# An RWKV attention with a token and channel mixer on one core: other costs in the planner, u turned by two wide transposes or by TensorE, and the row of w spread by a matmul

## The chip, the cores and the metric

The kernel runs on one core of a Trainium2 chip. The metric is the device time of one execution in microseconds (us). The five engines of the core are TensorE (PE in the profile), VectorE (DVE), ScalarE (ACT), GpSimd (POOL) and SyncE (SP). Each has its own queue and works through it in order. SP computes nothing here: it issues DMAs. PSUM is the memory into which TensorE writes, SBUF the one from which the engines work.

## The reference

Two parts, the output of the first being the input of the second (4 batches, 8 heads, 768 tokens, 48 numbers a head, so 384 to a token):

```python
for t in range(S):                       # attention, per batch and head
    cur = einsum('bhd,bhe->bhde', u * kt, vt)
    y[:, :, t] = einsum('bhd,bhde->bhe', rt, state + cur)
    state = w * state + einsum('bhd,bhe->bhde', kt, vt)
...
h  = max(xt @ w_tok1, 0) @ w_tok2        # mixer over the tokens, xt: x with tokens last
u  = x + h.T
h2 = max(u @ w_ch1, 0) @ w_ch2           # mixer over the channels
out = u + h2
```

Two things bear the name u: the small input `u` (8 x 48) of the attention, and the tensor u = x + h.T of the mixer. "u turned" is the second: the channel mixer needs u with its 384 channels on the partitions.

## The kernel before

**Attention.** The recurrence is done in blocks of 128 tokens. A block of one batch is a *unit*; there are 24 of them, 6 to a batch, units 0 to 5 being batch 0. For a unit, k, r and v (192 KB each) are loaded by SP's queue (`load`). k and r are multiplied by powers of w (`kp`, `rp`, on POOL or DVE, by the tables `wn` and `wp`), v is cast on ACT (`vb`). Both products, held side by side in `kpr` (128 x 1024), have to be turned so that the head's numbers lie on the partitions: by TensorE for units 0 to 11 (`trk`, `trr`: four transposes each into PSUM, then the copy `rk` on ACT, 128 x 1024), by one DMA transpose from SP's queue for units 12 to 23 (`turn_unit`; the tuple `turned`). Then come the scores (`at`, 8 matmuls into two PSUM tiles), their masking (`AT`, on DVE; in units 0 to 5 the second half is first copied out by ACT, `raw`, and masked from SBUF, `ATr`), the diagonal (`pr` on DVE, `pg` on TensorE, `adgp`, `yd`), the state (`kv` on TensorE, `S`), the outputs (`yS`, `y` on TensorE) and their sum `x` on DVE.

**Mixer.** Once a batch has all its x: `hid` (12 matmuls), `hr`, `bk` (12 matmuls into `hT_ps`), `us` (u, six adds on DVE, tiles of 128 x 384), and u turned. In batch 0 (`pe_turn`) TensorE turns it (`tu`: three transposes to a block, `uT`: the copy out of PSUM); in batches 1 to 3 six DMA transposes to a batch, each 128 x 384, go out on SP's queue (`uTd`). Then for either half of the batch 36 matmuls `z` (into `z_ps`, their moving operand being the turned u, 384 columns in a row), the maximum `zr`, 36 matmuls `h` (into `h_ps`), the last sum `os` (tile `osb`) and the store. The four weights come by POOL's queue, each after a certain unit's `rp` (`wafter`).

**What sets the order.** `graph` lists all steps with the engines that could do each, the time that the step is planned to keep an engine busy and the time after which its result is seen, a rank, and what must come before it. `Plan.run` plays this forward: whenever an engine is free, the ready step of lowest rank is given to it. Steps are then emitted in the order of their planned starts, and every engine keeps that order (`tc.keep_in_program_order`). So planned costs change no computation; they decide which engine takes a step that two can do, and in which order each queue holds its work. A step that is late in fact holds up what stands behind it in its queue. The factor `cold` stretches the planned TensorE time of units 0 to 5 and of batch 0's `hid`.

**Start.** ACT's queue loads w, repeated on all partitions (`w_bc`, 192 KB); ACT makes from it lnw and the tables. TensorE runs eight matmuls on zeros (`idle_ps`, `warm=8`). SP loads k, r, v of unit 0 and then the rows of w and u as a small tile (`rows`), which a matmul turns (`wu`, in f32); then the loads of unit 1 follow.

All instructions have one line in the profile (L338, the wrapper that keeps the order), so groups are told apart by their tiles.

Of the kernel before, what the change touches and what calls it, by code (L numbers as in the profile page):

```python
# [13 lines left out]
f32 = mybir.dt.float32  # L14
# [9 lines left out]
T = 128  # L24
# [20 lines left out]
class Plan:  # L45
# [3 lines left out]
    def __init__(self, banks, busy_until, in_flight):  # L49
        self.steps, self.banks, self.busy_until, self.in_flight = [], banks, busy_until, in_flight  # L50
# [20 lines left out]
    def run(self):  # L71
# [5 lines left out]
        while todo:  # L77
# [4 lines left out]
            while again:  # L82
                again = False
                for s in sorted(open_, key=lambda s: (s.rank, s.ready)):
# [40 lines left out]


# [7 lines left out]
def graph(do, cfg):  # L134

    p = Plan(4, cfg.get("busy_until", dict(ACT=3.0, DVE=3.3, POOL=3.6)), cfg.get("in_flight", 8))
# [9 lines left out]
    tables = {0: p.add("tables0", [("ACT", 1.6, 1.75)], rank=-100, emit=do("tables", 0))}  # L146
    setup = tables[0]
    for g in (1, 2):
        tables[g] = p.add(f"tables{g}", [("ACT", 1.05, 1.2)], [setup], rank=g - 0.6, emit=do("tables", g))

    wu = p.add("wu", [("PE", 0.6, 0.8)], rank=0.05, emit=do("wu"))
# [16 lines left out]
    def weight(i, after):  # L168
        s = p.add(f"i:w{i}", [("POOL", 0.9, 1.0, True)], after, rank=-50, emit=do("weight", i))
        took = cfg.get("wtime", (3.3, 3.0, 7.0, 7.8))[i]  # L170
        wx[i] = p.transfer(f"x:w{i}", s, took, took + 1.0, -1.0)

    p.wait(wu, [loads["v", 0]])
# [3 lines left out]
    for u in range(NU):  # L177
# [10 lines left out]
        rp = p.add(f"rp{u}", [POOL2, DK], [loads["r", u], tab, old], rank=r + 0.1, emit=do("rp", u))  # L188
# [52 lines left out]
    for b in range(B):  # L241
# [9 lines left out]
        uT = []  # L251
        for c in range(C):
# [5 lines left out]
            else:  # L258
                s = p.add(f"i:uT{b}_{c}", [("SP", 1.25, 1.3)], [us], rank=-3000 + c, emit=do("uTd", b, c))
                uT.append(p.transfer(f"x:uT{b}_{c}", s, 0.4, 1.3, 0.0))  # L260
        for sg in range(2):
# [7 lines left out]
            for si in range(3):  # L269
# [5 lines left out]
                s = p.add(f"i:o{b}_{c}", [("SP", 0.35, 0.4)], [s], rank=-1500, emit=do("out", b, c))  # L275
                stores.append(p.transfer(f"x:o{b}_{c}", s, 0.6, 1.8, 0.0))
# [20 lines left out]
def kernel(  # L297
# [52 lines left out]
    u_bc = const.tile([128, dm], f32, name="u_bc") if wide else None  # L350
    act.preload_act_table_set("natural_log_exp_and_others")

# [4 lines left out]
    for _ in range(CFG.get("warm", 0)):  # L357
        pe.matmul(idle_ps, idle[:, 0:128], idle, start=True, stop=True)


    rows = const.tile([2 * HP, 2, P], f32, name="rows")
    dve.memset(rows, 1.0)
# [44 lines left out]
    def tables(eng, g):  # L407
        if g == 0:
            act.activation(lnw, w_bc, Ln)
        act.activation(wn[:, g, :], lnw, Exp, scale=iota[:, 1, g:g + 1])  # L410
        act.activation(wp[:, g, :], lnw, Exp, scale=iota[:, 0, g:g + 1])
# [295 lines left out]
```

## Time and profile before

| | |
|---|---|
| median of 3 runs | 188.04 us (187.84 to 188.58) |
| the profiled execution | 188.54 us, its span 186.8 us |
| TensorE busy | 160.3 us (86%), 1440 matmuls |
| DVE, ACT, POOL busy | 97.1, 85.5, 61.9 us |
| DMA | 27.38 MB, 147 GB/s on average |
| mean granted TensorE clock | 0.982 |

The span runs from the first to the last instruction; 1.74 us of the execution lie around it. A busy TensorE is one with a matmul in its pipe: back to back, the 384-column matmuls start closer together than the duration that the profile gives for one. In a timeline row the first number is the start in us, the second the time to the end of the last instruction of the row; what stands in square brackets is the idle time of the engine before the row and what ended it. SPq is SP's queue, where the time of a row is that of issuing.

### The profile page before, as it was taken

What the parts mean: (1) busy time and instruction counts of PE and PEld (TensorE: products, weight loads), DVE (VectorE), ACT (ScalarE), POOL (GpSimd) and SP (SyncE); (2) the same over time, 40 slices, a digit from 0 to 9 for tenths busy, and PEclk for the clock granted to TensorE, in tenths of its full rate; (3) what the DMA queues carried; (4) which work ended last, traced back from release to release, by engine and by line L of the source; (5) the groups of instructions that cost most, each with busy time, mean ns of one, the idle gap of its engine ahead of it and who ended that gap; (6) DMA issues with size and microseconds to landing.
All of it is one profiled execution on the core that took longest, in us unless ns stands there. A gap on an engine that the chain in (4) does not pass through costs nothing.

```text
span 186.8 us, 3768 instructions
## 1 busy us (share of the span) xinstructions
PE 160.3 (86%) x1440; PEld 99.1 (53%) x1440; DVE 97.1 (52%) x199; ACT 85.5 (46%) x183; POOL 61.9 (33%) x77
## 2 busy tenths in 40 slices
PE   7458778799999999658979899974999999999992
PEld 2346555365666666434546454542656566556650
DVE  3279965650289877951834678734526702102121
ACT  2868555189538642017332473120551290652800
POOL 4208700044087699330185456511501000000000
PEclk9999999999999999979999999998799999999999
DMA  4899999999769899946899999749631352302103
GB/s 96 161 219 215 190 204 200 186 201 214 149 165 197 170 216 159 204 80 125 181 190 208 208 204 241 130 82 210 159 58 42 63 67 91 120 0 88 42 2 126
DMA packets 101690, 27.38 MB, mean 147 GB/s; under 512 B 95528, under 2 KB 101288, under 8 KB 101672
## 3 DMA queue, kind: packets, MB, share of 16 engines
q1 hardware_dynamic: 98520, 23.80, 62.6%
q0 software_dynamic: 3008, 3.15, 10.2%
q10 hardware_dynamic: 144, 0.20, 0.5%
q8 instruction: 11, 0.18, 0.4%
q14 instruction: 7, 0.06, 0.1%
HBM read 20.65 MB, written 4.72 MB: 136 GB/s over the span
## 4 chain that ended last, share of the span: by engine, by line
PE 53%; DVE 13%; DMA 12%; SPq 6%; issue 6%; ACT 4%; POOL 4%; POOLq 0%; DVEq 0%; ACTq 0%
PE h_ps L338 21%; PE z_ps L338 21%; SPq L338 6%; DMA ld_k<-in_k_dram 4%; DVE AT L338 3%; DMA ld_r<-in_r_dram 3%; PE hT_ps L338 3%; PE y_ps L338 3%; POOL kpr L338 2%; DMA ld_v<-in_v_dram 2%; DVE x_b L338 2%; DVE u_sb L338 2%; ACT rk L338 2%; PE at_ps L338 2%; PE tr_ps L338 2%
## 5 line engine op out<-in xcount | busy, mean ns | idle before, releaser
L338 ACT ACTIVATE zr<-z_ps 128x384 bf16<-128x384 f32 x95 | 46.2, 491 | 35.8 <-PE z_ps L338 35.7
L338 PE MATMUL z_ps<-uT,wch 128*128 128x384 bf16 x288 | 56.4, 337 | 1.6 <-DMA uT<-u_sb 1.6
L338 PE MATMUL h_ps<-wch,zr 128*128 128x384 bf16 x288 | 55.2, 326 | 0.0
L338 PEld LDWEIGHTS <-wch 128*128 128x128 bf16 x288 | 27.6, 100 | 19.4 <-issue 4.2
L338 PEld LDWEIGHTS <-zr 128*128 128x128 bf16 x288 | 26.6, 97 | 15.6
L338 POOL TENSOR_TENSOR yd<-vb,adg 128x384 f32<-128x384 bf16 x19 | 15.7, 828 | 45.3 <-ACT adg L338 44.9
L338 DVE TENSOR_TENSOR osb<-u_sb,h_ps 128x384 f32<-128x384 bf16 x24 | 13.0, 550 | 33.8 <-PE h_ps L338 33.7
L338 POOL TENSOR_TENSOR kpr<-ld_k,wn 128x384 bf16<-128x384 f32 x21 | 21.3, 1015 | 24.0 <-DMA ld_k<-in_k_dram 18.7
L338 DVE TENSOR_TENSOR AT<-at_ps,mask 128x512 bf16<-128x512 f32 x42 | 27.6, 683 | 2.1 <-PE at_ps L338 1.9
L338 POOL TENSOR_TENSOR kpr<-ld_r,wp 128x384 bf16<-128x384 f32 x20 | 20.6, 1028 | 9.1 <-DMA ld_r<-in_r_dram 5.7
L338 DVE TENSOR_TENSOR pr<-rk 128x512 bf16<-128x512 bf16 x24 | 12.2, 512 | 15.0 <-DMA rk<-kpr 11.3
L338 DVE TENSOR_TENSOR x_b<-y_ps,yd 128x384 bf16<-128x384 f32 x24 | 13.3, 553 | 11.8 <-PE y_ps L338 6.8
L338 PEld LDWEIGHTS <-kpr 128*128 128x128 bf16 x176 | 13.5, 113 | 9.7 <-DVE kpr L338 3.4
L338 PEld LDWEIGHTS <-rk 48*128 48x128 bf16 (+1 forms) x272 | 11.1, 101 | 14.0 <-DMA rk<-kpr 6.4
L338 ACT CAST vb<-ld_v 128x384 bf16<-128x384 f32 x24 | 12.2, 510 | 12.7 <-DMA ld_v<-in_v_dram 12.7
L338 ACT COPY rk<-tr_ps 128x1024 bf16<-128x1024 bf16 x12 | 12.1, 1010 | 9.6 <-PE tr_ps L338 7.6
L338 PE MATMUL at_ps<-rk 48*128 48x128 bf16 x192 | 10.6, 237 | 5.2 <-DMA rk<-kpr 4.1
L338 PE MATMUL tr_ps<-ident,kpr 128*128 128x128 bf16 x96 | 11.9, 265 | 2.7 <-DVE kpr L338 2.3
L338 DVE TENSOR_TENSOR S<-kv_ps,bm 128x384 bf16<-128x384 f32 x13 | 7.2, 553 | 13.1 <-PE kv_ps L338 10.6
L338 PE MATMUL h_ps<-x_b,wtok 128*128 128x384 bf16 x48 | 12.4, 348 | 1.5 <-DVE x_b L338 1.5
L338 DVE TENSOR_TENSOR u_sb<-x_b,hT_ps 128x384 bf16<-128x384 bf16 x24 | 11.9, 550 | 1.5 <-PE hT_ps L338 1.5
L338 PEld LDWEIGHTS <-wtok 128*128 128x128 bf16 x96 | 8.8, 100 | 6.9 <-issue 2.6
(58 smaller groups left out, 109.1 us busy)
## 6 DMA issues: line engine op xcount, KB each, us to landing
ld_k<-in_k_dram SPq DMA_DIRECT2D x24, 192.0 KB, 3.6
ld_r<-in_r_dram SPq DMA_DIRECT2D x24, 192.0 KB, 4.0
ld_v<-in_v_dram SPq DMA_DIRECT2D x24, 192.0 KB, 3.7
out_dram<-osb SPq DMA_DIRECT2D x24, 192.0 KB, 2.0
wch<-in_moe_w_ch_dram POOLq DMA_DIRECT2D x2, 1152.0 KB, 14.4
wtok<-in_moe_w_tok_dram POOLq DMA_DIRECT2D x2, 384.0 KB, 6.6
uT<-u_sb SPq DMA_TRANSPOSE x18, 2.4
w_bc<-in_w_dram ACTq DMA_DIRECT2D x1, 192.0 KB, 3.9
```

What stands on the lines that cost most here:

```text
L338: return lambda *args, **kw: tc.keep_in_program_order(f(*args, **kw))
```

## The change

- **Planned costs.** A load's issue costs SP 0.60 us in the plan (0.45 before) and its transfer 1.01 us, seen after 2.1 (0.93, 1.9); the transfers of a unit's DMA transpose, of the weights and of the stores get other times as well. ACT, DVE and TensorE are planned busy until 3.85, 3.6 and 5.0 us. `cold` is 1.7 in place of 1.0. The tables are split into single steps (`lnw`, `wn`, `wp`), and `rp` waits for `wp` alone.
- **Batch 0.** `raw` is empty: both halves of the scores are masked on DVE straight from PSUM. Weights are issued after units 4, 5, 5, 5 (3, 4, 5, 5 before).
- **u turned.** In batch 1 by TensorE, as in batch 0 (`pe_turn=(0, 1)`). In batches 2 and 3 by two DMA transposes to a batch, each of 128 x 1152 (half a batch). The tile `uT` is laid out by blocks, so the 384 columns that a `z` matmul reads are three pieces of 128, 384 apart.
- **Units 12 and 13** are turned by TensorE (`turned=range(14, 24)`).
- **Start.** w comes as one row (1.5 KB) on one partition and is spread by a matmul in f32 with a row of ones (`w_ps`, 128 x 384); lnw reads PSUM. The `rows` are issued on ACT's queue ahead of its table load. Two matmuls on zeros stand ahead of `w_ps` and ten behind it.
- A function `fill` is added, and not used with this `CFG`.

```diff
-    p = Plan(4, cfg.get("busy_until", dict(ACT=3.0, DVE=3.3, POOL=3.6)), cfg.get("in_flight", 8))
+    p = Plan(4, cfg.get("busy_until", dict(ACT=3.85, DVE=3.6, POOL=3.6, PE=5.0)), cfg.get("in_flight", 8))
...
-                s = p.add(f"i:{nm}{i}", [("SP", 0.45, 0.6)], fetched[-1:], rank=-1000 + n, emit=do("load", nm, i))
+                s = p.add(f"i:{nm}{i}", [("SP", 0.6, 0.65)], fetched[-1:], rank=-1000 + n, emit=do("load", nm, i))
...
-                loads[nm, i] = p.transfer(f"x:{nm}{i}", s, 0.93, 1.9, 0.0)
+                loads[nm, i] = p.transfer(f"x:{nm}{i}", s, 1.01, 2.1, 0.0)
...
-            s = p.add(f"i:t{u}", [("SP", 1.25, 1.3)], [kp, rp], rank=-2000, emit=do("turn_unit", u))
-            rk = p.transfer(f"x:t{u}", s, 1.0, 2.2, 0.0)
+            s = p.add(f"i:t{u}", [("SP", 1.35, 1.4)], [kp, rp], rank=-2000, emit=do("turn_unit", u))
+            rk = p.transfer(f"x:t{u}", s, 1.56, 2.2, 0.0)
...
-                s = p.add(f"i:uT{b}_{c}", [("SP", 1.25, 1.3)], [us], rank=-3000 + c, emit=do("uTd", b, c))
-                uT.append(p.transfer(f"x:uT{b}_{c}", s, 0.4, 1.3, 0.0))
+                some.append(us)
+                if c % G == G - 1:
+                    s = p.add(f"i:uT{b}_{c}", [("SP", 1.35, 1.4)], some, rank=-3000 + c, emit=do("uTd", b, c // G))
+                    uT += [p.transfer(f"x:uT{b}_{c}", s, 1.75, 2.4, 0.0)] * G
+                    some = []
...
-    wafter={0: 3, 1: 4, 2: 5, 3: 5},
+    wafter={0: 4, 1: 5, 2: 5, 3: 5},
     hold={6: ("rp", 5)},
-    turned=range(12, 24),
-    raw=range(6),
+    turned=range(14, 24),
+    pe_turn=(0, 1),
     kr0=0.2, yd0=0.1,
-    cold=1.0,
-    warm=8,
+    cold=1.7,
...
-    w_bc = const.tile([128, dm], f32, name="w_bc")
-    act.dma_start(out=w_bc, in_=w.rearrange("h d -> (h d)")[None, :].to_broadcast([128, dm]))
+    row = const.tile([1, 2, dm], f32, name="row")
+    rows = const.tile([2 * HP, 2, P], f32, name="rows")
+    dve.memset(rows, 1.0)
...
+            act.dma_start(out=row[:, j, :], in_=src.rearrange("h d -> (h d)")[None, :])
+    for j, src in enumerate((w, u)):
+        act.dma_start(rows[j * HP:j * HP + HP, :, 0:D], src.rearrange("(a q) d -> a q d", q=2))
...
+    warm(CFG.get("warm", (2, 10))[0])
+    pe.matmul(w_ps, ones, row[:, 0, :], start=True, stop=True)
+    warm(CFG.get("warm", (2, 10))[1])
...
-            for j, src in enumerate((w, u)):
-                sp.dma_start(rows[j * HP:j * HP + HP, :, 0:D], src.rearrange("(a q) d -> a q d", q=2))
...
-    def uTd(eng, b, c):
-        sp.dma_start_transpose(M[b]["uT"][:, :, ts(c, 128)], M[b]["u"][:, c, :])
+    def uTd(eng, b, sg):
+        half = slice(sg * G, sg * G + G)
+        sp.dma_start_transpose(M[b]["uT"][:, half].rearrange("p c m t -> p (c m) t"),
+                               M[b]["u"][:, half].rearrange("p c n -> p (c n)"))
...
-            pe.matmul(M[b]["z", sg, j], wch1[:, m, ts(j, 128)], M[b]["uT"][:, m, ds(sg * 384, 384)],
+            pe.matmul(M[b]["z", sg, j].rearrange("p (c t) -> p c t", c=G), wch1[:, m, ts(j, 128)], M[b]["uT"][:, sg * G:sg * G + G, m, :],
```

## Rows read from the trace of the kernel before

**Rows 1.** The page, part 2: TensorE's busy tenths in 40 slices of the span

```profile
PE   7458778799999999658979899974999999999992
```

**Rows 2.** Windows: length, busy us of PE, PEld, DVE, ACT, POOL, granted clock, DMA share, GB/s

```profile
76.70:82.30 5.60, 2.15 (x37) 1.39 (x36) 4.93 (x10) 0.33 (x2) 2.61 (x3) 0.93 0.67 139
82.30:88.00 5.70, 5.49 (x32) 2.95 (x32) 0.56 (x1) 3.55 (x8) 0.00 (x0) 0.77 0.55 106
88.00:95.00 7.00, 4.78 (x68) 3.27 (x69) 4.27 (x8) 2.88 (x8) 2.07 (x3) 1.00 0.85 175
95.00:124.50 29.50, 28.11 (x279) 16.65 (x277) 19.35 (x38) 10.30 (x26) 16.24 (x18) 1.00 0.97 189
124.50:133.00 8.50, 5.00 (x46) 2.70 (x43) 3.00 (x7) 2.13 (x5) 1.65 (x2) 0.80 0.88 189
133.00:183.20 50.20, 50.01 (x341) 30.03 (x337) 13.76 (x27) 22.23 (x47) 2.79 (x4) 1.00 0.24 64
```

**Rows 3.** Timeline of TensorE, 82 to 95 us

```profile
82.34 2.08 PE L338 MATMUL z_ps<-uT,wch 128*128 128x384 bf16 x6 [1.56 <-DMA uT<-u_sb]
84.56 3.27 PE L338 MATMUL z_ps<-uT,wch 128*128 128x384 bf16 x18
...
94.74 0.33 PE L338 MATMUL kv_ps<-vb,kpr 128*128 128x96 bf16 x4 [1.64 <-ACT vb L338]
```

**Rows 4.** Timeline of SP's queue, 77 to 128 us

```profile
77.27 7.71 SPq L338 DMA_TRANSPOSE uT<-u_sb  x6
...
88.96 0.70 SPq L338 DMA_DIRECT2D ld_v<-in_v_dram  x1
...
116.91 8.33 SPq L338 DMA_TRANSPOSE uT<-u_sb  x6
125.34 2.63 SPq L338 DMA_TRANSPOSE rk<-kpr  x2
```

**Rows 5.** Timeline of TensorE, 128 to 132 us

```profile
128.62 0.40 PE L338 MATMUL at_ps<-rk 48*128 48x128 bf16 x8 [3.44 <-DMA rk<-kpr]
...
129.37 3.08 PE L338 MATMUL z_ps<-uT,wch 128*128 128x384 bf16 x9
```

**Rows 6.** The chain that ended last, at 148 us: start, length, what

```profile
148.49 5.36 PE z_ps L338 x33
```

**Rows 7.** Timeline of TensorE, transposes between other matmuls, 58 us

```profile
57.93 0.40 PE L338 MATMUL tr_ps<-ident,kpr 128*128 128x128 bf16 x4
58.16 0.65 PE L338 MATMUL z_ps<-uT,wch 128*128 128x384 bf16 x3
```

**Rows 8.** Timeline of the start: SP's queue and TensorE, 1 to 8 us

```profile
1.27 3.60 PE L338 MATMUL idle_ps<-idle 128*128 128x512 bf16 x8 [1.27 <-DVE idle L338]
...
1.95 2.65 SPq L338 DMA_DIRECT2D ld_v<-in_v_dram  x1
...
6.20 0.45 SPq L338 DMA_DIRECT2D ld_k<-in_k_dram  x1
...
7.55 0.56 PE L338 MATMUL wu_ps<-ident_f,rows 8*128 8x8 f32 x2 [2.68 <-DMA rows<-in_u_dram]
```

**Rows 9.** Groups by form: the masking of scores and its copy (count, busy, mean ns)

```profile
L338 DVE TENSOR_TENSOR AT<-at_ps,mask 128x512 bf16<-128x512 f32 x42 | 27.6, 683 | 2.1 <-PE at_ps L338 1.9
...
L338 ACT CAST raw<-at_ps 128x512 bf16<-128x512 f32 x6 | 3.5, 587 | 1.3 <-PE at_ps L338 1.2
L338 DVE TENSOR_TENSOR AT<-raw,mask_b 128x512 bf16<-128x512 bf16 x6 | 2.5, 424 | 0.2 <-ACT raw L338 0.2
```

**Rows 10.** Timeline of TensorE: the same eight matmuls at 27 and at 31 us

```profile
27.17 0.61 PE L338 MATMUL at_ps<-rk 48*128 48x128 bf16 x8 [0.68 <-ACT rk L338]
...
31.13 0.40 PE L338 MATMUL at_ps<-rk 48*128 48x128 bf16 x8 [0.23 <-ACT rk L338]
```

**Rows 11.** Timeline of TensorE: four matmuls of two columns, and the next row

```profile
110.40 0.24 PE L338 MATMUL kv_ps<-UW,pr 128*128 128x2 bf16 x4
110.50 0.65 PE L338 MATMUL z_ps<-uT,wch 128*128 128x384 bf16 x3
```

More of the change, by code (lines that the diff above doesn't have):

```diff
@@ L110, in run @@
                         banks[i], held[s.name] = float("inf"), i
+                        self.used.append([now, float("inf"), s.name])
                     for g in s.give:
                         banks[held.pop(g)] = s.seen
+                        next(x for x in self.used if x[2] == g)[1] = s.seen
                         heapq.heappush(times, s.seen)
@@ L124, in run, with fill @@
         return sorted(self.steps, key=lambda s: s.start)
+    def fill(self, until, least, margin, each, emit):
+        mine = sorted((s for s in self.steps if s.engine == "PE"), key=lambda s: s.start)
+        for a, b in zip(mine, mine[1:]):
+            if b.start > until:
+                break
+            taken = sum(1 for x in self.used if x[0] < b.start and x[1] > a.end)
+            n = int((b.start - a.end - margin) / each)
+            if b.start - a.end >= least and taken < self.banks and n > 0:
+                s = self.add(f"fill{a.name}", [("PE", n * each, n * each)], emit=emit(n))
+                s.engine, s.start, s.end, s.seen = "PE", a.end, a.end + n * each, a.end + n * each
+        return sorted(self.steps, key=lambda s: s.start)
 MM = 0.1625
@@ L169, in weight @@
         s = p.add(f"i:w{i}", [("POOL", 0.9, 1.0, True)], after, rank=-50, emit=do("weight", i))
-        took = cfg.get("wtime", (3.3, 3.0, 7.0, 7.8))[i]
+        took = cfg.get("wtime", (3.0, 2.6, 6.2, 7.7))[i]
         wx[i] = p.transfer(f"x:w{i}", s, took, took + 1.0, -1.0)
-    p.wait(wu, [loads["v", 0]])
     wafter = cfg["wafter"]
@@ L274, in graph @@
                 downs[-1].append(s)
[L275 to L276 removed]
+                s = p.add(f"i:o{b}_{c}", [("SP", 0.57, 0.6)], [s], rank=-1500, emit=do("out", b, c))
+                stores.append(p.transfer(f"x:o{b}_{c}", s, 0.63, 1.8, 0.0))
     rng = random.Random(cfg.get("seed", 0))
@@ L356, with warm @@
     idle_ps = psM.tile([128, 512], f32, name="idle_ps", tag="m")
[L357 to L362, printed above, removed]
+    w_ps = psM.tile([128, dm], f32, name="w_ps", tag="m")
+    def warm(n):
+        for _ in range(n):
+            pe.matmul(idle_ps, idle[:, 0:128], idle, start=True, stop=True)
+    warm(CFG.get("warm", (2, 10))[0])
+    pe.matmul(w_ps, ones, row[:, 0, :], start=True, stop=True)
+    warm(CFG.get("warm", (2, 10))[1])
+    if wide:
+        u_ps = psM.tile([128, dm], f32, name="u_ps", tag="m")
+        pe.matmul(u_ps, ones, row[:, 1, :], start=True, stop=True)
     iota_i = const.tile([128, 2, G], i32, name="iota_i")
@@ L405, with lnw_, wn_, wp_ @@
     wGm = const.tile([128, HP, 2, D], f32, name="wGm")
-    def tables(eng, g):
-        if g == 0:
-            act.activation(lnw, w_bc, Ln)
+    def lnw_(eng):
+        act.activation(lnw, w_ps, Ln)
+    def wn_(eng, g):
         act.activation(wn[:, g, :], lnw, Exp, scale=iota[:, 1, g:g + 1])
+    def wp_(eng, g):
         act.activation(wp[:, g, :], lnw, Exp, scale=iota[:, 0, g:g + 1])
@@ L422, in uw @@
             dve.tensor_mul(UW[half, :, q], wu_sb[half, 0, :], wu_sb[half, 1, :])
+        if wide:
+            dve.tensor_copy(u_bc, u_ps)
     wtok1 = wts.tile([128, 6, dtok], bf16, name="wtok1")
@@ L627, in uT @@
     def uT(eng, b, c):
[L628 removed]
+        to = M[b]["uT"][:, c]
         if eng == "ACT":
@@ L662 @@
     STEPS = {
-        "tables": tables, "wu": wu, "uw": uw, "load": load, "weight": weight, "gd": gd, "wGm": wgm, "kp": kp, "rp": rp,
+        "lnw": lnw_, "wn": wn_, "wp": wp_, "wu": wu, "uw": uw, "load": load, "weight": weight, "gd": gd, "wGm": wgm, "kp": kp, "rp": rp,
         "vb": vb, "ku": ku, "rku": rku, "adg": adg, "yd": yd, "turn_unit": turn_unit,
@@ L672, in do, with fill @@
         return lambda eng: STEPS[kind](eng, *args)
-    for s in graph(do, CFG).run():
+    def fill(eng, n):
+        t = psM.tile([128, 256], f32, name="fill_ps", tag="m")
+        for _ in range(n):
+            pe.matmul(t, idle[:, 0:128], idle[:, 0:256], start=True, stop=True)
+    plan = graph(do, CFG)
+    steps = plan.run()
+    if CFG.get("fill"):
+        first = next(s for s in steps if s.name == "z0_0_0").start
+        steps = plan.fill(first, *CFG["fill"], lambda n: lambda eng: fill(eng, n))
+    for s in steps:
         if s.emit is not None:
```

27 lines of the change are left out of this document (15 added, 12 removed).

## The prediction

> **What bounds the kernel now.** I read first the page's row of TensorE by slices [rows 1]: the reader sees a start of mixed digits, nines from slice 9 on, then two dips, in slices 17 to 21 and in 27 and 28 (a slice is 4.67 us), and nothing but nines from slice 29 until the stores. So TensorE is the bound from about 40 us on, except in those dips; nothing that shortens another engine's work elsewhere can pay. Then I asked for windows around the dips [rows 2]. From 95.0 to 124.5 us TensorE is idle for 1.39 us, from 133.0 to 183.2 for 0.19. From 76.7 to 95 it is idle for 3.45 + 0.21 + 2.22 = 5.88 us, from 124.5 to 133 for 3.50. After each dip the granted clock falls (0.77 and 0.80 as means of the windows), so TensorE is busy and slow there. Last I asked the timelines of TensorE and of SP's queue who ends these waits [rows 3 to 5].
>
> The unit price comes from a stretch without waits: 33 z matmuls in 5.36 us, 0.162 each [rows 6]; the profile's duration of a group is longer by the pipe's drain, 0.65 - 3 x 0.162 = 0.16 us [rows 7].
>
> *First dip (batch 1).* SP issues six transposes of u in a row, 7.71 us, 1.29 each [rows 4]. The first z waits 1.56 us for one [rows 3]. Behind the six stand loads: v that is issued at 88.96 us [rows 4] is what ACT waits for, and TensorE through it, 1.64 us at 94.74 [rows 3]. The 24 z that follow the hole take 2.08 + 3.27 = 5.35 us where 24 x 0.162 + 2 x 0.16 = 4.22 would do: 1.13 lost to the lower clock. Lost in all: 5.88 + 1.13 = 7.0 us.
>
> *Second dip (batch 2).* Again six transposes, 8.33 us, and behind them, at 125.34, two transposes of units [rows 4]; TensorE waits 3.44 us for such a one, and the next nine z take 3.08 us where 9 x 0.162 + 0.16 = 1.62 would do [rows 5]. Lost: 3.50 idle and 1.46 at the lower clock, 5.0 us.
>
> *Batch 3* has six such transposes too, but TensorE is full from 133 us on [rows 2], so they cost nothing.
>
> **The change, part by part.**
>
> *u of batch 1 and units 12 and 13 on TensorE.* Removed from SP: six transposes and two of units, some 10 us of its queue; the loads behind move up by that. Added to TensorE: 18 transposes for u and 16 for the units. Four take 58.16 - 57.93 = 0.23 us of TensorE's time [rows 7], 0.057 each, so 34 x 0.057 = 1.9 us, all on the path, as TensorE is the bound there. Added to ACT: six copies of u and two of 128 x 1024. The nearest row for a copy out of PSUM is 0.587 us for 128 x 512 [rows 9], so 6 x 0.587 + 2 x 1.17 = 5.9 us at most; ACT is idle for 18.3 - 6.8 = 11.5 us of this stretch [rows 2], which hides them. If the plan gives them to DVE there is no such cover: DVE works 4.93 of 5.6 us from 76.7 on [rows 2]. DVE is therefore the next late one once SP is out of the way, and I take not all of the 7.0 but 6.2 (what DVE has free in that window, 0.67, is about what I leave). Ends: 3.5 (only the hole before the first z goes) and 7.0.
>
> *Two wide transposes.* A transpose of a unit moves eight blocks of 128 x 128 and costs SP 2.63/2 = 1.32 us; one of u moves three and costs 8.33/6 = 1.39 [rows 4]. So an issue does not grow with its blocks up to eight, and nine should cost about 1.4: two cost 2.8 us in place of 8.33, and the transposes of units behind them are issued 5.5 us sooner. That is more than the 3.44 us wait that they end, so the hole closes, and the clock does not fall after it. The wide one must wait for three sums u where the narrow one waited for one, and holds all of SP's queue meanwhile: two more operations on DVE, at most 2 x 0.683 [rows 9] = 1.4 us; 5.5 - 1.4 still covers 3.44. I take 4.5 of 5.0; ends 0 (something else arrives late at the same place) and 5.0. Batch 3: nothing, as above.
>
> *Batch 0.* w_bc's 192 KB leave the first loads' way, and two small issues leave SP's queue. Now v of unit 0 takes 2.65 us to issue and the next load comes at 6.20, 1.6 us after that issue ends [rows 8]. The 1.6 are certain; about 2 of the 2.65 may go as well, if w_bc held it up. So units 1 to 5 are loaded 1.6 to 3.6 us sooner. Against it: without `raw` DVE has 6 x (0.683 - 0.424) = 1.6 us more to do in batch 0, ACT 3.5 less [rows 9]; and ten matmuls on zeros stand ahead of unit 0's transposes in TensorE's order. Eight take 3.6 us [rows 8], ten 4.5, behind a spread of w that can't start before its row has landed. The nearest row for that is the small tile's, for which TensorE waits until 7.55 [rows 8]; issued first on ACT it should be there at about 3 us. The f32 matmul of 384 columns lies between 0.28 (half the 0.56 of the two f32 records [rows 8]) and some 2 us (12 x 0.16). So TensorE is free for unit 0 between 7.8 and 9.5 us; now it is at 8.1 (7.55 + 0.56). I take a gain of 1.0 for the start; ends -2.0 and +3.6.
>
> *Costs in the plan.* They change order, not work. What order can still give is the idle time outside the dips, 1.4 us between 95 and 124.5 [rows 2]; what it can take away I bound by the same amount. Weights one unit later and the split tables: within the same bound. I take 0. That the whole first batch is planned 1.7 times slower agrees with the trace: eight scores take 0.61 us at 27 us and 0.40 at 31 [rows 10], and less pipe's drain the ratio is nearer two, so this stretch runs at the lower of the two clock levels (1.2 and 2.4 GHz).
>
> The rule of the Trainium skill that speaks against moving turns to TensorE is in its page "TensorE: Matmul & The Clock Gate", Part 4 (PE-mode transpose): a transpose does not count as activity for the clock as a matmul does. By it, the clock would fall around u of batch 1 and the 1.13 us of rows 3 would stay, 179.3 in place of the forecast. The trace is against it as far as it goes: z right behind transposes runs at its full rate there [rows 7].
>
> **Sum.** 1.0 + 6.2 + 4.5 - 1.9 = 9.8 us. The rows come from an execution of 188.54 us (span 186.8 and 1.74 around it), 0.50 above the median of the runs; a gain is the same against either, so 188.04 - 9.8 = 178.2 us.
>
> **Rivals.**
>
> 1. *The second hole stays.* From 95 to 124.5 the DMA engines are already at a share of 0.97 [rows 2]. If loads for units 18 to 23, wanted some 5 us sooner, can't come sooner, TensorE waits for them where it waited for the transpose. For it: that share; a wide transpose moves the same bytes. Against: between 76.7 and 95 the shares are 0.67, 0.55, 0.85 [rows 2], room for 5.6 x 0.33 + 5.7 x 0.45 + 7 x 0.15 = 5.5 us of transfers. Time: 178.2 + 4.5 = 182.7.
> 2. *The clock is up in batch 0.* If twelve matmuls on zeros that run on into unit 0 without a gap raise the clock and the work behind holds it, each TensorE step of batch 0 is 0.21 us shorter [rows 10]; four steps (transposes, scores, two for y) lie in the chain of each of the last three units, 12 x 0.21 = 2.5 us, and with the loads' whole 3.6 in place of 1.0: 178.2 - 2.5 - 2.6 = 173.1. Against: today's eight matmuls are followed by a wait of 2.68 us [rows 8] and steps at the lower level until 27 us and beyond [rows 10], with TensorE busy most of that time [rows 1]. The Trainium skill's same page says in Part 1 (the HAM clock gate) that sustained activity releases the clock and gaps take it back; that would favour this rival, and no row shows twelve without a gap.
> 3. *The plan does not do what it says.* DVE, full in the first dip, takes the hole's place, and unit 0 starts at the late end: 188.04 - (4.5 - 1.9 - 2.0) = 187.4, no change that can be told.
> 4. *Slower: z reads its moving operand in three pieces.* If each of the two breaks costs what a matmul of two columns costs, (110.50 - 110.40)/4 = 0.025 us [rows 11], 288 z cost 288 x 2 x 0.025 = 14.4 us, nearly all where TensorE is the bound: 178.2 + 14.4 = 192.6. It outweighs the gain from 9.8/288 = 0.034 us a matmul. For it: no row shows a moving operand in pieces of this kind. Against: a break is no instruction of its own, and below 0.034 us the sign stays.
>
> **How the numbers follow.** Forecast 0.50, rival 1 0.20, rival 2 0.15, rival 3 0.06, rival 4 0.09. The range leaves out rivals 3 and 4 and the outermost 5 in 100: 173.5 to 184.0 (rival 1 with another 1.3 of order). About 0.5% is what a measurement of this kernel can tell from no change: faster 0.85, the same 0.06, slower 0.09.
>
> **What would show it.** Right: between bk and z of batch 1 no idle TensorE and no fall of the clock; two transposes of u in batch 2 in SP's queue at about 1.4 us each, and no wait of over 1 us for rk<-kpr; z still 0.162 apart. Rival 1: a wait of some 3 us for loads in batch 2 or 3. Rival 2: scores of units 1 to 4 in 0.40 us. Wrong altogether: z over 0.19 apart, or the first z of batch 0 later than it is now.

## The result and the profile after

| | before | after |
|---|---|---|
| median of four | 188.31 us (187.84 to 188.86) | 180.13 us (176.14 to 183.55) |
| the profiled execution, its span | 188.54, 186.8 us | 183.46, 181.8 us |
| first `z` of batch 0 starts at | 38.57 us | 47.07 us |
| from there to the end of the last `h` | 144.5 us | 130.9 us |
| last `h` to the end of the span | 3.7 us | 3.8 us |
| TensorE busy, matmuls | 160.3 us, 1440 | 160.6 us, 1480 |

Forecast were 178.2 us and a range of 173.5 to 184.0. The changed kernel's five executions (the median is of four of them) fall into two groups, three at 176.1 to 177.4 us and two at 183.5; its ratio to before, 0.939 (0.933 to 0.944), is of the shorter group, as the ratios below are of the shorter executions of each kernel, and the traces that exist are of the longer one. The median lies between the groups, where none of these executions is. The table tells at once that two large things of opposite sign lie in the 5.1 us between the two profiled executions: the start lost 8.5 us, and what follows gained 13.6.

The page after, TensorE's busy tenths and its granted clock in 40 slices, answers to [rows 1]:

```profile
PE   6969693038999999999999999999999999999991
PEclk9975858558999999999999999999999999999999
```

The dips in slices 17 to 21 and 27 and 28 are gone. Nines run from slice 11 on. A new hole, "303", stands in slices 7 to 9 (a slice is now 4.55 us), where there was none.

Windows of after (columns as in [rows 2]):

```profile
28.90:39.42 10.52, 0.01 (x2) 0.01 (x1) 0.00 (x0) 0.00 (x0) 1.04 (x2) 0.65 1.19 191
39.42:47.07 7.65, 6.80 (x46) 3.41 (x46) 3.85 (x8) 2.43 (x6) 3.68 (x4) 0.81 1.04 192
47.07:84.00 36.93, 36.38 (x411) 23.84 (x411) 23.47 (x46) 24.20 (x47) 19.79 (x21) 1.00 0.75 154
84.00:95.00 11.00, 11.00 (x121) 7.33 (x120) 9.14 (x20) 7.28 (x20) 7.28 (x8) 1.00 1.11 197
95.00:109.70 14.70, 14.50 (x152) 8.92 (x150) 10.45 (x20) 5.16 (x15) 9.18 (x10) 1.00 1.03 214
109.70:133.00 23.30, 23.21 (x235) 14.41 (x233) 16.01 (x31) 11.63 (x30) 8.14 (x11) 1.00 0.82 161
133.00:178.00 45.00, 45.00 (x303) 27.03 (x300) 12.44 (x25) 18.24 (x38) 1.61 (x2) 1.00 0.21 62
```

In the first window no engine but POOL does anything for 10.5 us, while the DMA engines are full. From 47.07 us to the end of the last `h` TensorE is idle for 0.55 + 0 + 0.20 + 0.09 + 0 = 0.84 us, and the granted clock reads 1.00. In the kernel before it was idle for 11.45 us between the first `z` and the end of the last `h`.

The timeline of TensorE after names the hole:

```profile
28.43 0.48 PE L357 MATMUL y_ps<-S,rk 128*128 128x96 bf16 x4
39.42 0.61 PE L357 MATMUL tr_ps<-ident,kpr 128*128 128x128 bf16 x4 [10.51 <-POOL kpr L357]
39.82 0.85 PE L357 MATMUL h_ps<-x_b,wtok 128*128 128x384 bf16 x2
...
47.07 0.65 PE L357 MATMUL z_ps<-uT,wch 128*128 128x384 bf16 x3
47.72 7.07 PE L357 MATMUL z_ps<-uT,wch 128*128 128x384 bf16 x42
```

TensorE stands before the four transposes of a `kpr`: those of unit 6, the first of batch 1. Behind them in its queue wait the last matmuls of batch 0's `hid` (`h_ps<-x_b,wtok`), which need nothing of unit 6. The chain that ended last in after (start, length, what) says what the transposes wait for:

```profile
24.07 14.17 DMA ld_k<-in_k_dram
38.38 0.99 POOL kpr L357
39.42 0.61 PE tr_ps L357 x4
```

It is the load of unit 6's k: 14.17 us for 192 KB, where the loads of k land after 3.7 us as a median. The timelines of POOL's queue and of SP's queue in after show the company it has:

```profile
22.46 0.76 POOL L357 DMA_DIRECT2D wtok<-in_moe_w_tok_dram  x1
23.22 1.80 POOL L357 DMA_DIRECT2D wch<-in_moe_w_ch_dram  x2
```

```profile
24.07 0.37 SPq L357 DMA_DIRECT2D ld_k<-in_k_dram  x1
...
25.47 8.78 SPq L357 DMA_DIRECT2D ld_v<-in_v_dram  x1
```

384 + 2 x 1152 KB of weights are issued around it, from 1.6 us ahead of it to 1.0 us after. The same happens before (k of unit 6 is issued at 28.08 us there), but there its transposes stand behind batch 0's `z` in TensorE's order, so that nobody waits for it.

Why the order differs can be read from the plan itself, in its own clock. Before, the plan placed the transfer of unit 6's k behind all the weights and its transposes at 42.0, after batch 0's `hid` (27.7). In the changed plan a free slot opened just ahead of the second weight: transfer from 22.7 to 23.7, `trk` at 26.7, ahead of the last three steps of batch 0's `hid` (27.0, 27.9 and 28.7). The plan believed in a load 1 us long that took 14. The costs didn't open the slot by themselves. Played forward with the weights back at their old units, or with `cold` back at 1.0, the changed plan puts the transfer at 38.3 or 39.0 and the transposes at 42.0 or 42.3, behind `hid` again; neither was run on the chip.

Where the 13.6 us behind the first `z` come from: TensorE's idle time falls by 11.45 - 0.84 = 10.6 us, the 1.13 + 1.46 = 2.6 us lost to the lower clock behind the two dips [rows 3, 5] come back, the new transposes cost 34 x 0.057 = 1.9, and some 0.7 us of small work moved ahead of the first `z`. That is 10.6 + 2.6 - 1.9 + 0.7 = 12.0; the other 1.6 us lie in rows counted as busy and can't be put down to single rows.

### The profile page after: what moved, and what is told of

Its sections match the earlier page's. It is cut to its first block, busy times and chain, and to the rows that moved or that the text cites. A ratio compares the mean times of both kernels' runs of the same rounds, so it can differ in the third digit from the quotient of the medians.

```text
span 181.8 us, 3810 instructions
## 1 busy us (share of the span) xinstructions
PE 160.6 (88%) x1480; PEld 99.1 (55%) x1480; DVE 97.6 (54%) x198; ACT 85.2 (47%) x183; POOL 65.1 (36%) x81
## 4 chain that ended last, share of the span: by engine, by line
PE 70%; DMA 12%; DVE 6%; issue 4%; POOL 4%; ACT 1%; SPq 1%; DVEq 0%; POOLq 0%
PE h_ps L357 27%; PE z_ps L357 26%; DMA ld_k<-in_k_dram 8%; PE hT_ps L357 4%; PE y_ps L357 4%; POOL kpr L357 3%; PE kv_ps L357 3%; PE at_ps L357 3%; DMA ld_r<-in_r_dram 2%; DMA ld_v<-in_v_dram 2%; PE tr_ps L357 2%; DVE pr L357 2%; DVE x_b L357 1%; PE t_ps L357 1%; DVE AT L357 1%
## 5 line engine op out<-in xcount | busy, mean ns | idle before, releaser
L357 PE MATMUL z_ps<-uT,wch 128*128 128x384 bf16 x288 | 53.6, 326 | 0.2
L357 POOL TENSOR_TENSOR yd<-vb,adg 128x384 f32<-128x384 bf16 x22 | 18.2, 827 | 50.1 <-ACT adg L357 43.2
L357 DVE TENSOR_TENSOR AT<-at_ps,mask 128x512 bf16<-128x512 f32 x48 | 31.4, 684 | 8.7 <-PE at_ps L357 8.6
L357 PEld LDWEIGHTS <-wch 128*128 128x128 bf16 x288 | 26.9, 98 | 16.2 <-issue 0.7
L357 PEld LDWEIGHTS <-zr 128*128 128x128 bf16 x288 | 26.7, 98 | 15.4
L357 DVE TENSOR_TENSOR osb<-u_sb,h_ps 128x384 f32<-128x384 bf16 x24 | 13.1, 553 | 32.9 <-PE h_ps L357 32.8
L357 POOL TENSOR_TENSOR kpr<-ld_r,wp 128x384 bf16<-128x384 f32 x21 | 21.5, 1021 | 6.3 <-ACT wp L357 3.5
L357 PE MATMUL tr_ps<-ident,kpr 128*128 128x128 bf16 x112 | 12.5, 243 | 11.7 <-POOL kpr L357 10.5
L357 DVE TENSOR_TENSOR x_b<-y_ps,yd 128x384 bf16<-128x384 f32 x24 | 13.3, 553 | 15.8 <-PE y_ps L357 14.5
L357 PEld LDWEIGHTS <-kpr 128*128 128x128 bf16 x192 | 12.7, 104 | 15.2 <-POOL kpr L357 11.3
L357 ACT COPY rk<-tr_ps 128x1024 bf16<-128x1024 bf16 x14 | 14.2, 1011 | 10.6 <-PE tr_ps L357 10.5
L357 DVE TENSOR_TENSOR pr<-rk 128x512 bf16<-128x512 bf16 x24 | 13.7, 573 | 0.2 <-ACT rk L357 0.2
L357 PE MATMUL h_ps<-x_b,wtok 128*128 128x384 bf16 x48 | 13.6, 372 | 0.1
L357 DVE TENSOR_TENSOR S<-kv_ps,bm 128x384 bf16<-128x384 f32 x13 | 7.2, 553 | 10.6 <-PE kv_ps L357 10.5
L357 ACT COPY adg<-kv_ps 128x8 f32<-128x8 f32 x20 | 3.3, 166 | 18.0 <-PE kv_ps L357 17.5
```

Of the source, the lines that this page charges most:

```text
L357: return lambda *args, **kw: tc.keep_in_program_order(f(*args, **kw))
```

## The experiments

Questions: what makes the hole, and what would the kernel be without it (e1, e13, e2, e9)? What is each part of the change worth by itself (e3, e4, e5, e11, e12), and what is it worth where the order is right (e8, e6, e10)? The theory on the hole is that the load's late arrival and the order together make it; the rival, that batch 0's `z` would have to wait for its weights anyway, since they share the DMA engines with that load. Of each run the table gives the median, its range, and the ratio to the kernel before on the same chip with its interval; e1 and e13 repeat the changed kernel and have none.

| run | us | ratio to before |
|---|---|---|
| e1, after again | 183.91 (179.44 to 184.45) | |
| e13, after again, one execution | 183.9 | |
| e2, unit 6's k late in the plan | 173.72 (172.15 to 174.60) | 0.921 (0.914 to 0.927) |
| e9, unit 6's k loaded early | 172.63 (172.56 to 172.84) | 0.912 (0.910 to 0.915) |
| e3, before + wide transposes | 178.02 (177.80 to 178.61) | 0.945 (0.942 to 0.948) |
| e4, before + u of batch 1, units 12, 13 on TensorE | 181.68 (179.13 to 182.83) | 0.956 (0.948 to 0.963) |
| e11, before + both | 177.67 (177.24 to 180.09) | 0.942 (0.934 to 0.949) |
| e5, before + new start | 188.19 (183.97 to 191.40) | 0.979 (0.971 to 0.987) |
| e12, before + both + new start | 178.82 (176.78 to 179.37) | 0.945 (0.935 to 0.955) |
| e8, e2 with u of batch 1 by DMA | 178.40 (177.36 to 179.12) | 0.944 (0.939 to 0.949) |
| e6, e2 with narrow transposes | 174.36 (172.83 to 175.24) | 0.920 (0.915 to 0.926) |
| e10, e9 without the ten matmuls on zeros | 171.78 (170.27 to 172.91) | 0.908 (0.900 to 0.917) |

### e1 and e13: the changed kernel again

No edit.

> The changed kernel as it is, to see an execution of it whose span is near 175 us beside the one of 181.8. Theory A (arrival): the two differ in when the first load of unit 6 lands, so in the 175 us execution TensorE's wait ahead of unit 6's transposes is about 4 us and not 10.5, and the first z of batch 0 starts near 40.5 us and not at 47.1; from there on the two agree within 0.5 us. Theory B (clock): the first z starts at the same 47 us in both, and the 6.7 us lie behind it.

> The changed kernel as it is, once more, for a trace of a shorter execution. Theory A (arrival): the span and the landing of unit 6's first load move together: from the first z to the last h 130.9 us as in the first trace (47.1 to 178.0), within 0.7, and what the span differs by from 181.8 is what the first z differs by from 47.1. Theory B (clock): the first z stays at 47 us and the span differs behind it.

Both profiles are again of the longer kind, with the same hole. TensorE in e1:

```profile
39.07 0.61 PE L357 MATMUL tr_ps<-ident,kpr 128*128 128x128 bf16 x4 [10.83 <-POOL kpr L357]
```

It is no accident of one execution: three traces have a wait of 10.5 to 10.8 us at the same instruction (10.63 in e13). From the first `z` to the end of the last `h` all three take 130.9 us. In e1 and e13 the first `z` comes 0.4 us later than in after (47.50 and 47.48), and the span is 0.4 us longer: what these three differ by lies ahead of the first `z`. What the shorter executions look like, no trace shows; one of e1's, 179.44 us, lies between the two groups.

### e2: unit 6's k late in the plan

```diff
+    p.wait(loads["k", 6], [wx[3]])
+    loads["k", 6].rank = -0.5
     rng = random.Random(cfg.get("seed", 0))
```

Only the plan is told that this transfer comes after the last weight. Work and loads are the same but for one step that goes from ACT to DVE; the order of the queues is what changes.

> The changed kernel with one thing told to the plan: unit 6's first load is seen only after the last weight has landed. No wait is added on the chip, only orders change. Theory A (order): TensorE's hole of 10.5 us at 28.9 is unit 6's transposes standing ahead of batch 0's last hid in TensorE's queue; with them behind, the first z starts at 35 to 37 us and the time is 170 to 172 us. Theory B (weights): z would wait for its weights anyway, which are issued at 23.2 us; the first z then starts at 40 us or later, with TensorE waiting for the DMA of a weight, and the time is 175 us or more.

173.72 us, above theory A's 170 to 172, with the first `z` where theory A has it. TensorE's row of the page, and its timeline at the first `z`, in e2:

```profile
PE   6968979779999899999999999999999999999991
```

```profile
36.43 0.66 PE L359 MATMUL z_ps<-uT,wch 128*128 128x384 bf16 x3 [1.09 <-DMA wch<-in_moe_w_ch_dram]
```

The hole is gone. The rival is right on 1.09 us of the 10.5: so long the first `z` does wait for its weights. The other 9.4 were order. From the first `z` to the end of the last `h` this order takes 132.7 us, 1.8 more than after, about as much as the time lies above theory A's upper end.

### e9: unit 6's k loaded early

```diff
-        if i in CFG.get("hold", {}) and nm == CFG.get("lorder", "krv")[0]:
-            first = INS[CFG["hold"][i]]
+        if i == 7 and nm == CFG.get("lorder", "krv")[0]:
+            first = INS["rp", 5]
```

The other side of the theory: plan and order stay as in the changed kernel, but the loads that are held back until unit 5's `rp` begin with unit 7, not unit 6.

> The changed kernel with all its orders as they are; what makes unit 6's transposes wait is taken away: the wait that holds SP's queue until unit 5's rp stands ahead of unit 7's loads in place of unit 6's, so unit 6 is loaded ahead of the weights. Theory A (arrival: the hole of 10.5 us is that load, landing behind 2 MB of weights, and the spread from 176 to 184 us is the spread of its landing): TensorE waits less than 2 us ahead of those transposes, the first z comes at 36 to 39 us, the time is 172.5 to 175.5 and the runs lie within 1.5 us. Theory B (the order itself is slow, whenever the load lands): the time stays at 179 or more.

172.63 us. SP's queue, then TensorE, then a window (columns as in [rows 2]) of e9:

```profile
16.84 1.89 SPq L357 DMA_DIRECT2D ld_k<-in_k_dram  x1
```

```profile
28.65 0.39 PE L357 MATMUL tr_ps<-ident,kpr 128*128 128x128 bf16 x4
...
35.94 0.66 PE L357 MATMUL z_ps<-uT,wch 128*128 128x384 bf16 x3 [0.68 <-DMA wch<-in_moe_w_ch_dram]
```

```profile
35.94:167.40 131.46, 130.28 (x1212) 81.49 (x1212) 71.15 (x136) 66.06 (x145) 47.51 (x52) 1.00 0.73 146
```

With k issued 7.2 us sooner the same transposes, in the same place of the same order, wait for nothing. From the first `z` to the end of the last `h` it is 131.5 us, about as in after (130.9): the difference of 10.7 us in span (181.8 - 171.1) lies ahead of the first `z`, and the hole was 10.5. So it takes both, the order and the late arrival, and either mends it. The four executions of e9 lie within 0.28 us, those of after within 7.4. That points to the landing of this one load as what parts the two groups; it isn't shown, for want of a trace of the shorter one. The shorter executions of after lie only 3.5 to 4.8 us above e9's median, so the hole can't have cost 10.5 us in them.

### e3: the kernel before with wide transposes

```diff
     def uTd(eng, b, c):
-        sp.dma_start_transpose(M[b]["uT"][:, :, ts(c, 128)], M[b]["u"][:, c, :])
+        if c % G == G - 1:
+            half = slice(c - G + 1, c + 1)
+            sp.dma_start_transpose(M[b]["uT"][:, half].rearrange("p c m t -> p (c m) t"),
+                                   M[b]["u"][:, half].rearrange("p c n -> p (c n)"))
```

with `uT` laid out by blocks, and `z` reading three pieces. Here batch 1 is turned by wide transposes too; plan and order are those of before.

> The kernel before, in its own order, with one part of the change: u of batches 1 to 3 turned by two wide transposes to a batch, issued where the third and the sixth narrow one stood. By the prediction's step the second dip closes (4.5 to 5.0 us), and the first one loses some 5 us of SP's queue as well: 178 to 183 us. The rival (something else late at the same place) gives 186 to 188. Three pieces in z's moving operand cost nothing if z stay 0.162 us apart; at 0.19 apart the time is 188 or more.

178.02 us, a gain of 10.5 on the 188.51 of before on its chip: more than this part was given in the forecast, and by itself more than the forecast's whole sum of 9.8. SP's queue, windows (columns as in [rows 2]) and TensorE in e3:

```profile
76.52 2.71 SPq L338 DMA_TRANSPOSE uT<-u_sb  x2
...
110.96 3.99 SPq L338 DMA_TRANSPOSE uT<-u_sb  x2
```

```profile
76.00:83.00 7.00, 5.06 (x66) 3.11 (x65) 6.49 (x13) 1.10 (x4) 3.09 (x4) 1.00 1.10 213
83.00:173.20 90.20, 88.35 (x740) 53.71 (x738) 43.83 (x80) 40.29 (x91) 22.87 (x25) 1.00 0.61 127
```

```profile
82.82 3.09 PE L338 MATMUL z_ps<-uT,wch 128*128 128x384 bf16 x18
```

2.71 us of SP's queue in place of 7.71 [rows 4] end most of the first dip too, and 3.99 in place of 8.33 the second: in this order SP's queue, held by six issues, made the second dip and most of the first. In the first window DVE works 6.49 of 7 us and TensorE still idles for 1.9. That part was never SP's. Of the 3.45 us that TensorE idles in before from 76.7 to 82.3 [rows 2], waits for DVE take 0.74 + 0.35 + 0.40 + 0.39 = 1.88 and the wait for a transpose of u 1.56. The first of them in before:

```profile
77.88 0.25 PE L338 MATMUL kv_ps<-UW,pr 128*128 128x2 bf16 x4 [0.74 <-DVE pr L338]
```
The last row of e3 prices the moving operand in three pieces: (3.09 - 0.16)/18 = 0.163 us, as in one piece [rows 6]. Rival 4 has no ground.

### e4 and e11: u of batch 1 and units 12 and 13 on TensorE, and both parts

```diff
-    turned=range(12, 24),
+    turned=range(14, 24),
+    pe_turn=(0, 1),
```

> The kernel before with one part of the change: u of batch 1 and units 12 and 13 turned by TensorE, the plan's costs as before. By the prediction's step the first dip closes (7.0 us, 6.2 taken) for 1.9 us of transposes: 183 to 184 us, with the second dip (3.4 us of waiting for a unit's transpose) still there. If the order made with the old costs is what loses, the time stays at 186 to 188.

e11 has this and the edit of e3.

> The kernel before with its old costs and old start, and both parts that concern u: batch 1's u and units 12 and 13 on TensorE, wide transposes for batches 2 and 3. If the two parts add where they don't overlap, the first dip (7.0 us) and the second (5.0) go for 1.9 us of transposes: 188.3 - 10.1 = 178.2 us, no better than wide ones alone (178.0). If TensorE's turning closes what the wide ones leave in the first dip (some 2 us of waits at 77 to 82 us), 175 to 177.

e4 gains 6.8 us by the medians (188.51 to 181.68) and 8.4 by the ratio, more than the 4.5 to 5.5 expected; the first dip goes and the second stays, with a wait at its old place. TensorE in e4:

```profile
118.60 0.61 PE L339 MATMUL at_ps<-rk 48*128 48x128 bf16 x8 [2.71 <-DMA rk<-kpr]
```

Together they gain 10.8 us (188.44 to 177.67), where apart they gain 10.5 + 6.8 = 17.3. The two parts are two ways to much of the same gain in batch 1. What TensorE's turning does there once the wide ones are in, the window of e11 shows beside that of e3 above (columns as in [rows 2]):

```profile
76.00:83.00 7.00, 7.00 (x81) 4.66 (x79) 5.93 (x14) 4.66 (x11) 5.05 (x6) 1.00 1.09 205
```

It does fill the 1.9 us that e3 leaves idle. But from the first `z` to the end of the last `h` TensorE is idle for 1.1 us less than in e3 (3.3 against 4.4) and busy for 1.3 us more (130.7 against 129.4): in the old order this part pays for its transposes and no more.

### e5 and e12: the new start

Both take w as one row, spread by a matmul, `rows` on ACT's queue and 2 + 10 matmuls on zeros; e5 has nothing else, e12 has it on top of e11:

```diff
-    act.dma_start(out=w_bc, in_=w.rearrange("h d -> (h d)")[None, :].to_broadcast([128, dm]))
+    act.dma_start(out=row[:, 0, :], in_=w.rearrange("h d -> (h d)")[None, :])
...
-            act.activation(lnw, w_bc, Ln)
+            act.activation(lnw, w_ps, Ln)
```

> The kernel before, in its own order and costs, with the new start alone: w as one row spread by a matmul, the small rows issued by ACT, two and ten matmuls on zeros. By the prediction's step the start gains 1.0 us (ends -2.0 and +3.6): first z of batch 0 at 36 to 38 us in place of 38.6, time 186.5 to 187.5. In the changed kernel's trace the first hid comes at 25.4 us, 2.6 us sooner than before; if the start alone does that, the time is 185.5 to 186.5. If ten matmuls on zeros hold up unit 0, or the order waits on something else, 188 or more.

> The run with both parts of u and the old costs, with the new start besides. If the start is worth what the first z shows in the changed kernel once unit 6 is early (35.9 us against 38.6), the time is some 2.5 us below the run without it. If loads that come sooner gain nothing in an order made for later ones, as in the kernel before with the new start alone (first z at 38.5 us), the two agree within 1 us, and the gain at the start belongs to the new costs.

TensorE's first `z` in e5:

```profile
38.52 0.65 PE L338 MATMUL z_ps<-uT,wch 128*128 128x384 bf16 x3
```

It is 38.57 in before. In e12 the first `z` is at 38.38, in e11 at 37.81. By this mark alone the new start gives nothing in the old order, and the whole time of e5 spreads over 7 us and decides nothing. But the mark hides a gain. TensorE at batch 0's `bk`, in before and then in e5:

```profile
35.44 1.53 PE L338 MATMUL hT_ps<-h1r,wtok 128*128 128x384 bf16 x8 [0.42 <-ACT h1r L338]
```

```profile
33.97 2.79 PE L338 MATMUL hT_ps<-h1r,wtok 128*128 128x384 bf16 x8 [0.26 <-ACT h1r L338]
```

e5 is there 1.47 us sooner, and the same eight matmuls take 1.26 us more: their granted clock is 0.50, in before 1.00. The start isn't what lowers it, for e3 and e4 have 0.50 there too, with the old start; e12 has 0.50 and e11 1.00. Of the four at 0.50, the two with the new start have their first `z` at 38.52 and 38.38 (e5, e12), the two with the old one at 39.47 and 39.93 (e3, e4): with the clock alike the new start gains 0.9 to 1.6 us, on two traces to a side. The 2.6 us in e9 (38.57 - 35.94) need the new order or `raw` as well; which of these wasn't told apart. And e12, which has everything but the costs, the split tables, `raw` and the weights' units, has no hole: the hole came with these.

### e8 and e6: the two parts in the right order

e8 is e2 without `pe_turn=(0, 1)`; e6 is e2 with each wide transpose issued as three narrow ones at the same place in the order:

```diff
-    pe_turn=(0, 1),
```

```diff
-        sp.dma_start_transpose(M[b]["uT"][:, half].rearrange("p c m t -> p (c m) t"),
-                               M[b]["u"][:, half].rearrange("p c n -> p (c n)"))
+        for c in range(sg * G, sg * G + G):
+            sp.dma_start_transpose(M[b]["uT"][:, c], M[b]["u"][:, c, :])
```

> The kernel with unit 6's load late in the plan (173.7 us), and u of batch 1 turned by two wide transposes like that of batches 2 and 3, TensorE turning that of batch 0 alone. By the prediction's step TensorE was needed to close the first dip: a wait of 2 us or more for a transpose of u in batch 1, 176 to 178 us. The rival, from the kernel before with wide transposes alone at 178.0: wide ones close that dip too, and TensorE is spared 18 transposes, 1.0 us: 172.5 to 174.5.

> The kernel with unit 6's load late in the plan (173.7 us), in the same order, but each wide transpose of u (batches 2 and 3) issued as three narrow ones at its place. By the prediction's step this brings the second dip back: SP is held some 5.5 us longer in batch 2, TensorE waits 3 us for a unit's transpose and slows down after it, 177 to 179 us. The rival: with the first dip gone TensorE has other work at that place and nothing is late, 173.5 to 175.

e8 loses 178.40 - 173.72 = 4.7 us (4.4 by the two ratios, as the chips differ). Its windows (columns as in [rows 2]) and TensorE:

```profile
76.00:82.00 6.00, 2.82 (x37) 1.70 (x36) 5.65 (x11) 0.75 (x3) 2.86 (x4) 0.94 1.07 214
82.00:90.00 8.00, 8.00 (x74) 4.92 (x72) 3.57 (x8) 5.05 (x11) 2.27 (x4) 0.83 0.93 180
```

```profile
78.33 0.25 PE L358 MATMUL kv_ps<-UW,pr 128*128 128x2 bf16 x4 [1.58 <-DVE pr L358]
...
80.34 0.33 PE L358 MATMUL y_ps<-S,rk 128*128 128x96 bf16 x4 [0.73 <-DVE x_b L358]
```

TensorE idles for 3.2 of 6 us and is slow after that, and what it waits for is DVE, full for 5.65 of the 6; the wait for a transpose of u that was expected isn't there. It is a hole that the wide transposes left and that TensorE's own turning fills with work: e2 idles for 0.2 us from 76 to 83.

In e6 the rival came out. It takes 0.6 us more than e2, less than the spread of either, and has the same ratio to before; six issues in a row are back in its SP queue:

```profile
103.69 9.06 SPq L359 DMA_TRANSPOSE uT<-u_sb  x6
```

9.06 us of the queue, and from there to 167 us the view of waits lists none for TensorE. In this order the narrow transposes cost no more than the wide ones: nothing that stands behind them in the queue comes late for TensorE.

### e10: without the ten matmuls on zeros

```diff
-    warm(CFG.get("warm", (2, 10))[1])
+    warm(0)
```

on top of e9.

> The kernel with unit 6 loaded early (172.6 us), without the ten matmuls on zeros behind the spread of w. Theory C (they serve the clock): units 0 and 1 then run at the lower clock level from the start, scores at 0.61 us in place of 0.40 at 11 us, and the first z comes 0.5 to 1.5 us later: 173 to 174. Theory D (they only stand in the way): unit 0's transposes start at 6 us in place of 8.5, and the time is the same or up to 1 us less.

171.78 us, 0.85 less than e9 by the medians (on another chip; 0.75 by the ratios), in a range that holds e9's. TensorE and one window of e9, then of e10 (columns as in [rows 2]):

```profile
13.59 0.40 PE L357 MATMUL at_ps<-rk 48*128 48x128 bf16 x8
16.57 0.61 PE L357 MATMUL at_ps<-rk 48*128 48x128 bf16 x8
```

```profile
14.50:28.00 13.50, 11.64 (x142) 8.82 (x141) 12.49 (x23) 6.87 (x13) 10.46 (x12) 0.51 1.06 179
```

```profile
9.84 0.61 PE L357 MATMUL at_ps<-rk 48*128 48x128 bf16 x8 [0.23 <-ACT rk L357]
...
15.42 0.61 PE L357 MATMUL at_ps<-rk 48*128 48x128 bf16 x8 [0.18 <-ACT rk L357]
...
34.99 0.66 PE L357 MATMUL z_ps<-uT,wch 128*128 128x384 bf16 x3 [0.21 <-DMA wch<-in_moe_w_ch_dram]
```

```profile
14.50:28.00 13.50, 12.04 (x140) 9.01 (x139) 12.29 (x22) 6.84 (x14) 10.31 (x12) 1.00 1.09 188
```

By these durations the clock is at its upper level at 13.6 us in e9 and at its lower one by 16.6. In e10 the scores take 0.61 us from the first one, and the first `z` comes 0.95 us sooner. What the ten matmuls win is given back before batch 0 is over, and they stand ahead of unit 0. So the rise is real and, as far as these runs tell, worth nothing here. e10 and e9 are the fastest versions seen, and by their medians both are ahead of the changed kernel's shortest execution, by 3.5 us and more.

## Why the prediction was right or wrong

**The order, 0 (ends -1.4 and +1.4): wrong.** This is the step that failed, and it failed by its bound. I had argued that order can give no more than the idle time outside the dips, 1.4 us, and then bounded what it can take away "by the same amount". For a loss there is no such bound: the idle time that there is says how much can be won, and nothing about how much can be made. A load that is late by 10 us costs 10 as soon as a transpose of it is put ahead of work that is ready. In the profiled execution after it was 10.5, of which 9.4 were order (e2); in the shorter executions it can't have been more than some 5. "Weights one unit later", which I had put within the same bound, has a hand in it: with the weights at their old units the changed plan has no slot for that load.

**The start, +1.0 (ends -2.0 and +3.6): the mechanism right, the place hidden.** SP issues unit 1's k at 2.70 us where it was at 6.20 [rows 8], 3.5 us sooner, nearly the upper end, and unit 5's v at 15.47 for 17.90; `lnw` starts at 4.18 for 4.74. Alone, with the clock alike, the start brings the first `z` 0.9 to 1.6 us sooner (e5, e12 against e3, e4), near the 1.0 forecast; with the new order and without the hole it comes 2.6 us sooner (e9), with the hole 8.5 us later. No row stood behind the factor 12 in the upper bound for the f32 matmul; it measured 1.64 us. So one of the two signs for "wrong altogether", the first `z` later than now, did come, though the kernel got faster: the sign was a good one for the start and a bad one for the whole.

**u of batch 1 and units 12, 13, +6.2 - 1.9: right for this plan, with another reason.** From 84 to 95 us TensorE is busy for 11.00 of 11.00 us at a clock of 1.00. e4 gives 6.8 for the part alone, e8 4.7 within the changed kernel with its hole mended; 6.2 - 1.9 = 4.3 was forecast. But I took SP's queue for the whole cause in batch 1 and TensorE for the cure. The 5.88 idle us hold 1.88 that were waits for DVE already; e3 shows that a freed queue ends most of the rest as well, and e8 that what is left then is DVE's, which I had named as the next late one. The Trainium skill's page "TensorE: Matmul & The Clock Gate", Part 4 (PE-mode transpose), says that a transpose does not count for the clock as a matmul does, by which it would fall around these transposes. That did not come to bear here: the 18 transposes of u stand between matmuls from 85.0 to 89.6 us, and the granted clock in that window is 1.00. The total can't say anything of the 179.3, as the hole moved it.

**Two wide transposes, +4.5 (ends 0 and 5.0): right on the queue, an alternative and not an addend.** Nine blocks cost an issue of 1.4 us, as supposed, when they stand back to back; the timeline of SP's queue after, batches 2 and 3:

```profile
111.94 1.81 SPq L357 DMA_TRANSPOSE uT<-u_sb  x1
...
114.67 2.27 SPq L357 DMA_TRANSPOSE uT<-u_sb  x1
...
117.67 1.37 SPq L357 DMA_TRANSPOSE rk<-kpr  x1
...
141.87 2.74 SPq L357 DMA_TRANSPOSE uT<-u_sb  x2
```

4.08 us in place of 8.33 in batch 2 [rows 4], with loads between the two; no wait for `rk<-kpr` is left. The second dip's 5.0 us are gone. In the old order this part is worth more than its upper end, 10.5 (e3), since it ends most of the first dip too. In the new one e6 loses nothing without it that can be told, which is the lower end, 0: the rest of the change closes that dip as well. I added terms that each were priced against the kernel before; e11 (10.8) against e3 and e4 (10.5 and 6.8) shows that they overlap.

**The sum.** In the profiled execution the parts behind the first `z` gave 13.6 where 6.2 + 4.5 - 1.9 = 8.8 were forecast, and the start took 8.5 where it should have given 1.0. That the forecast is close to the median is luck: a loss that I hadn't seen met a gain that I had taken too small, and the median stands between two groups of executions. With the hole mended the same change stands at 172.6 (e9). That is rival 2's time (173.1) and not rival 2: e9's clock in batch 0 rises and falls again, and a gain of 2.5 us from it isn't shown. What brings 172.6 is the stretch ahead of the first `z`, with 2.6 us in place of 1.0, and the one behind it, with 13.1 in place of 8.8: other waits of TensorE, idle time that I had left out as small, went as well.

**Rivals 1, 3 and 4.** No second hole: 0.09 us of idle time from 109.7 to 133. DVE, in e8 full for 5.65 of 6 us, didn't take the hole's place in after, where TensorE's turning put work there (e2 against e8). The three pieces cost nothing (e3). The slower side that I gave a price was the wrong mechanism; the one that came, a late load ahead of ready work in an in-order queue, was not on the list.

**What stays open.** What the shorter executions of the changed kernel look like; what decides at which clock level batch 0's `bk` runs in the old order; what of e9's 2.6 us is the order and what `raw`; and where 1.6 of the 13.6 us lie.

## What to carry to other kernels

Where a planner's costs set a static order, a change of costs is worth reading as an order: list what each in-order queue now holds ahead of work that is ready, and of each such step ask when its data land in the trace, not in the plan. The idle time of the profile, with what the lower clock behind it costs, bounds what a better order can win, never what a worse one can lose. And two cures of one wait are not two gains: price the second with the first in place, in the order that will run. Turning on TensorE was worth 6.8 us alone (e4), next to nothing beside wide transposes in the old order (e11), and u of batch 1 by itself 4.7 us beside them in the new one (e8).

## What the runs showed of the hardware that was not expected

- A load of 192 KB that is issued among 2.7 MB of weights on another queue took 14.17 us to land (3.7 as a median), and the next issue but one on SP's queue held the queue for 8.78 us. The Trainium skill, page "DMA: Bandwidth & Descriptors", section "Queues, rings and completion order", says that each DMA engine takes turns between its queues by the packet; a load of many small pieces that shares its turns with large ones would land late by that. No run here takes this mechanism apart.
- The granted clock reads 1.00 from 14.5 to 28 us in e10, with eight scores at 0.61 us; in e9, where the scores had first been at 0.40, it reads 0.51 for the same work. In these two the row shows the lower level only after a rise, so at the start of a span the level has to be read from durations.
- A DMA transpose of nine blocks of 128 x 128 holds SP's queue for 1.36 us where two stand back to back (2.71/2 in e3) and for up to 2.27 (after, batch 2), one of three blocks for 1.29 (7.71/6 in before) to 1.51 (9.06/6 in e6).
- The f32 matmul that spreads w, 384 columns, takes 1.64 us for its two records, within the 0.28 to 2 that were estimated. It lies under the loads of unit 0. TensorE's start in after:

```profile
2.50 1.64 PE L357 MATMUL w_ps<-row,ones 1*128 1x384 f32 x2
4.08 4.38 PE L357 MATMUL idle_ps<-idle 128*128 128x512 bf16 x10
8.38 0.38 PE L357 MATMUL wu_ps<-ident_f,rows 8*128 8x8 f32 x2
```
